# Both layers of a channel MLP by Strassen's seven block products on one Trainium2 core

## The chip, the cores and the metric

The kernel runs on 1 core of one Trainium2 chip. TensorE does the matrix products and the transposes, VectorE (DVE), ScalarE (ACT) and GpSimd (POOL) everything between them; SyncE (SP) issues every DMA. The metric is the device time of one execution in microseconds. Time before: 950.23 us, the median of 3 runs (949.29 to 950.75). What a measurement of this kernel can tell from no change is about 0.2%, some 2 us.

## The reference, cut to what matters

```python
# q, k, v: (4, 12, 448, 64); 4 * 448 = 1792 tokens of 12 * 64 = 768 numbers
x  = attention(rmsnorm(q), rmsnorm(k), v)             # softmax, 48 heads
h  = relu(x @ moe_w_in)                               # 768 -> 1024, split in u, v
x  = (u * (w_spatial @ norm(v) + b)) @ moe_w_out      # 512 -> 768
u  = x + token_mlp(x)                                 # over tokens, 448 -> 256 -> 448
h2 = relu(u @ moe2_w_ch1) @ moe2_w_ch2                # 768 -> 1536 -> 768
return u + h2
```

The weights arrive as 64-bit floats. The last but one line is the channel MLP that is changed.

## The kernel before, in words

Every product of full precision is made from three TensorE passes: each operand is split into a rounded high part and the remainder (`HI`, `LO`), and `PASSES` multiplies high by high, high by low and low by high.

A weight of 64 bits goes through `convert` (line 495 on): ACT takes the absolute value, DVE clamps, shifts and merges the two words in four instructions, ACT makes the high part and POOL subtracts it for the low part. Weights that are wanted more than once are converted early, by `prepare_uo` and `prepare_next`, in pieces of 128x256 beside the attention, and stored in scratch tensors (`wu_d`, `wo_d`, `w1_d`, `w2_d`, and two blocks each of the channel layers, `c1_d`, `c2_d`).

The stages: attention, 24 pairs of heads in slots of eight softmax maxima each (`nm`), with the gated MLP (`moe`) of the first three batches laid between; `moe` of the last batch with the first products over tokens; the token MLP (`Tokens`); and the channel MLP (`channels`). In `channels` the hidden layer is made in six groups of two blocks of 128 features. For each group and each of four token blocks (512, 512, 512, 256) `up` makes two hidden blocks (18 matmuls each, tile `h2ps`, split again by ACT and DVE), and `down` multiplies the previous ones by the second layer and adds them on DVE to sums of all 1792 tokens that stay in SBUF (`acc`, tile `o_ps`). Each group's weights are fetched as 64-bit words and converted in this stage (`word`, `c`).

The order of instructions on each engine is not written by hand. The kernel records operations (`Plan.add`) with an estimated cost (`Plan.estimate`), and `Plan.issue` places them with `Plan.place`: at each step the engine that comes free first takes its most urgent ready operation. Operations of DVE and POOL that need the SBUF port the two share (`op.port`) exclude one another there. `successors` opens new pools in SBUF when all users of the old ones are done (a fence).

Of the kernel before, what the change touches and what calls it, by code (L numbers as in the profile page):

```python
# [149 lines left out]
class Plan:  # L150
# [63 lines left out]
    def estimate(self, engine, fn, out, ins, kwargs):  # L214
# [30 lines left out]
        return max(475, size / 260), 2400 + 1.2e-3 * size  # L245
# [17 lines left out]
    def place(self, before, after, lag, weight, tiles=None):  # L263
# [21 lines left out]
        while placed < len(ops):  # L285
            t, e = min(
                (free_at[e] if waiting[e] else max(free_at[e], due[e][0][0]), e)
                for e in engines if waiting[e] or due[e])
            while due[e] and due[e][0][0] <= t:
                i = heapq.heappop(due[e])[1]  # L290
                heapq.heappush(waiting[e], (weight[i], i))
            i = heapq.heappop(waiting[e])[1]
            if e == "tensor" and ops[i].parts != parts:

                near = [x for x in waiting[e] if ops[x[1]].parts == parts and x[0] <= weight[i] + NEAR]
                if near:
# [4 lines left out]
                    i = x[1]  # L301
            if ops[i].port:
# [110 lines left out]
SWITCH, NEAR = 75, 2500  # L413

# [23 lines left out]
def attention_moe_mixer(  # L438
# [97 lines left out]
    c1_d = [scratch([P, 2, KD, P], F32R, f"c1_d{f}") for f in range(2)]  # L536
    c2_d = [scratch([P, 2, DM], F32R, f"c2_d{f}") for f in range(2)]
# [48 lines left out]
    class Attention:  # L586
# [131 lines left out]
        def divisors(self, i):  # L718
# [5 lines left out]
            wide = p.tile([T, 2 * C, D], F32, tag="wide", bufs=1, name="wide")  # L724
# [191 lines left out]
    def prepare_next(mp):  # L916
# [25 lines left out]
        n = NX // P  # L942
        for f in range(2):
            for j in range(0, KD, n):
                piece(
                    wdram(w_ch1)[j * P:(j + n) * P, f * P * W:(f + 1) * P * W].rearrange(
                        "(j p) f -> p j f", p=P), P, (n, P), c1_d[f][:, :, j:j + n])
                yield
        for f in range(2):
            for t in range(0, DM, NX):  # L950
                piece(wdram(w_ch2)[f * P:(f + 1) * P, t * W:(t + NX) * W], P, (NX,), c2_d[f][:, :, t:t + NX])
                yield
# [95 lines left out]
    class Tokens:  # L1048
# [6 lines left out]
        def prepare(self):  # L1055
            p = self.p
            self.w1 = p.tile([P, 2 * C - 1, DT], F32R, tag="w1", bufs=1, name="w1")
            self.w2 = p.tile([P, 2, KT, S], F32R, tag="w2", bufs=1, name="w2")
            self.w2r = p.tile([P, KT, 2, R], F32R, tag="w2r", bufs=1, name="w2r")
# [9 lines left out]
            fetch(self.w2, w2_d)  # L1069
            for kt in range(KT):  # L1070
                for a in (HI, LO):
                    fetch(self.w2r[:, kt, a], w2_d[:, a, kt, LAST:])
# [32 lines left out]
        def sums(self, b, n):  # L1105
            ns = slice(n * self.N, (n + 1) * self.N)
            for c, (t, m) in enumerate(TOK):
                ps = mm_tile("u_ps")[:, :self.N]
                x = self.x[b, c][:m, ns]
                if m == P:  # L1110
                    yield from run(
                        ps, [(self.w2[:, w, kt, t:t + m], self.h1[b, n, kt][:, a])
                             for kt in range(KT) for a, w in PASSES], 6)
                else:
                    yield from run(
                        ps, [(self.w2r[:, kt].rearrange("p a t -> p (a t)"), self.h1[b, n, kt][:, a])
                             for kt in range(KT) for a in (HI, LO)], 6)
                    two = self.p.tile([R, self.N], F32, tag="two", bufs=1, name="two")
# [5 lines left out]
        def turn(self, b, n, ut):  # L1124
            for j in range(n * KD // 2, (n + 1) * KD // 2):

                tp = psum.tile([P, C * P], "tp", "tp")
                for c, (t, m) in enumerate(TOK):
                    nc.tensor.transpose(tp[:, t:t + P], self.x[b, c][:, j * P:(j + 1) * P], ident)
                tpf = tp[:, :S]  # L1130
                bs = slice(b * S, (b + 1) * S)
# [10 lines left out]
    def channels(wp, cp, ut):  # L1142
        blocks = [(t0, min(512, NTOK - t0)) for t0 in range(0, NTOK, 512)]
        out_f = out.rearrange("b s d -> (b s) d")
        G = 2
        c1, c2 = {}, {}
        N = DM // 2

        def load_up(f):
            t = wp.tile([P, 2, KD, P], F32R, tag="c1", bufs=3, name="c1")  # L1150
            c1[f] = t
            if f < 2:
                nc.sync.dma_start(out=t.bitcast(F32), in_=c1_d[f].bitcast(F32))
                return
            for i in range(2):
                js = slice(i * KD // 2, (i + 1) * KD // 2)
# [147 lines left out]
    for _ in tokens():  # L1304
        pass
# [35 lines left out]
```

## Time and profile before

| | |
|---|---|
| median of 3 runs | 950.23 us (949.29 to 950.75) |
| span of the profiled execution, first to last instruction | 947.7 us, 2.5 us under that median |
| granted TensorE clock, mean | 0.996 |
| PE busy | 915.4 us, 97% of the span |
| DVE / ACT / POOL busy | 568.6 / 454.2 / 340.9 us |
| attention up to its last softmax maximum | 0 to 441.5 us |
| last batch's gated MLP, first token products | to 535.2 us |
| token MLP | to 595.5 us |
| channel MLP | to the end |

The span is that of one execution under the profiler; the profile gives no other time for it. Busy time is counted per engine, so one may be compared with the length of a stretch. A busy PE is not PE at its peak, since the ends of matmuls are modelled: the rate is read from long runs of one matmul in the chain of waits.

### The profile page before, as it was taken

To read this page: it belongs to the slowest core of one execution; us is meant where nothing else is said; L and a number is where in the kernel's file an instruction comes from. 1 tells how busy PE (TensorE), PEld (TensorE's weight loads), DVE (VectorE), ACT (ScalarE), POOL (GpSimd) and SP (SyncE) were. 2 spreads that over 40 slices of the span, in tenths; PEclk is the share of its full clock that TensorE was granted. 3 is DMA by queue.
4 is the path that set the end of the run, shared out by engine and by line. 5 is a ranking of instruction groups with operands and counts; after the bars stand their busy time and mean duration, and the time that the engine had idled before them with its cause. 6 is when DMAs were issued, how large, how long until landed. Compare 5 with 4: busy or idle time off the path is not lost.

```text
span 947.7 us, 15541 instructions
## 1 busy us (share of the span) xinstructions
PE 915.4 (97%) x5368; PEld 741.9 (78%) x5368; DVE 568.6 (60%) x1235; ACT 454.2 (48%) x1145; POOL 340.9 (36%) x501
## 2 busy tenths in 40 slices
PE   4897999999999999999999999999999999999998
PEld 2444467778667786677899999899899999999898
DVE  4888888876776666764151376634655556565434
ACT  5897887777776666675342344301312212122100
POOL 2566445685557654656044123101201102011100
PEclk9999999999999999999999999999999999999999
DMA  6455645557524565233764385721211112111024
GB/s 145 138 146 145 173 134 145 134 173 218 142 63 129 182 202 152 67 107 122 240 205 155 100 275 162 270 90 34 84 51 45 57 34 84 51 51 50 17 89 144
DMA packets 124654, 118.58 MB, mean 125 GB/s; under 512 B 74784, under 2 KB 108128, under 8 KB 123040
## 3 DMA queue, kind: packets, MB, share of 16 engines
q1 hardware_dynamic: 124576, 117.59, 41.2%
q8 instruction: 42, 0.69, 0.3%
q14 instruction: 36, 0.29, 0.1%
HBM read 89.77 MB, written 27.79 MB: 124 GB/s over the span
## 4 chain that ended last, share of the span: by engine, by line
PE 89%; ACT 4%; DMA 2%; DVE 2%; SPq 1%; issue 1%; POOL 0%; ACTq 0%; DVEq 0%; POOLq 0%
PE o_ps L406 19%; PE h2ps L406 18%; PE tp L406 10%; PE av L406 8%; PE sc L406 6%; PE xps L406 6%; PE ups L406 6%; PE vps L406 6%; PE sps L406 4%; PE u_ps L406 3%; PE h1ps L406 3%; ACT e L406 2%; SPq L406 1%; DVE wpart L406 1%; ACT et L406 1%
## 5 line engine op out<-in xcount | busy, mean ns | idle before, releaser
L406 PE MATMUL o_ps<-c,h 128*128 128x384 f32 x1008 | 179.8, 337 | 0.0
L406 PE MATMUL h2ps<-ut,c 128*128 128x512 f32 (+1 forms) x864 | 179.4, 364 | 0.0
L406 PEld LDWEIGHTS o_ps<-c,h 128*128 128x128 f32 x1008 | 175.0, 188 | 2.1 <-DVE acc L406 0.5
L406 PEld LDWEIGHTS h2ps<-ut,c 128*128 128x128 f32 x864 | 148.0, 189 | 24.1
L406 POOL TENSOR_TENSOR c<-word,c 128x384 fp32r<-128x384 f32 x40 | 40.6, 1014 | 271.7 <-ACT c L406 248.2
L406 ACT ACTIVATE e<-sc,nm 112x448 f32<-112x448 f32 x192 | 120.9, 640 | 36.4 <-PE tp L406 19.7
L406 DVE TENSOR_REDUCE nm<-sc 112x1 f32<-112x448 f32 x192 | 110.3, 615 | 41.4 <-PE sc L406 41.2
L406 PE MATMUL tp<-ident,e 112*128 112x112 f32 x672 | 96.2, 265 | 4.9 <-DVE et L406 2.6
L406 PEld LDWEIGHTS tp<-ident,e 112*128 112x128 f32 x672 | 74.1, 142 | 30.9 <-ACT et L406 7.8
L406 DVE TENSOR_TENSOR acc<-o_ps,acc 128x384 f32<-128x384 f32 x140 | 77.3, 555 | 29.5 <-PE o_ps L406 28.8
L406 POOL TENSOR_SCALAR e<-e,sums 112x448 f32<-112x448 f32 x112 | 70.7, 649 | 46.7 <-DVE sums L406 14.5
L406 ACT ACTIVATE c<-word 128x384 fp32r<-128x384 f32 x40 | 21.0, 525 | 128.3 <-DVE word L406 63.6
L406 ACT ACTIVATE h<-h2ps 128x512 fp32r<-128x512 f32 (+1 forms) x48 | 25.9, 539 | 111.6 <-PE h2ps L406 111.2
L406 DVE SCALAR_TENSOR_TENSOR h<-h2ps,h 128x512 fp32r<-128x512 f32 (+1 forms) x48 | 30.0, 625 | 80.6 <-ACT h L406 80.5
L406 ACT ACTIVATE et<-tp 128x448 f32<-128x448 f32 x120 | 65.5, 552 | 18.6 <-PE tp L406 16.8
L406 PE MATMUL ups<-xp,wu 128*128 128x448 f32 x288 | 70.2, 379 | 0.3 <-PE tp L406 0.3
L406 PE MATMUL av<-et,v 128*64 128x448 f32 x288 | 67.3, 564 | 0.2 <-DVE kt L406 0.2
L406 PE MATMUL xps<-wo,g 128*128 128x256 f32 x432 | 62.6, 291 | 0.4 <-ACT xo L406 0.4
L406 PEld LDWEIGHTS xps<-wo,g 128*128 128x128 f32 x432 | 55.0, 190 | 5.3 <-issue 1.3
L406 PEld LDWEIGHTS ups<-xp,wu 128*128 128x128 f32 x288 | 51.6, 188 | 8.3 <-issue 2.1
L406 PE MATMUL vps<-wv,xp 128*128 128x512 f32 x216 | 56.6, 405 | 1.0 <-ACT e L406 1.0
L406 DVE TENSOR_SCALAR word<-word 128x384 f32<-128x384 f32 (+2 forms) x92 | 33.7, 368 | 36.2 <-ACT word L406 34.3
(113 smaller groups left out, 1458.5 us busy)
## 6 DMA issues: line engine op xcount, KB each, us to landing
raw<-in_moe_w_ch_dram SPq DMA_DIRECT2D x40, 384.0 KB, 3.2
wu<-wu_d SPq DMA_DIRECT2D x16, 768.0 KB, 4.6
wo<-wo_d SPq DMA_DIRECT2D x12, 1024.0 KB, 5.1
raw<-in_q_dram SPq DMA_DIRECT2D x48, 112.0 KB, 2.8
acc<-u_d SPq DMA_DIRECT2D x14, 384.0 KB, 7.8
out_dram<-o SPq DMA_DIRECT2D x28, 192.0 KB, 1.9
v<-in_v_dram SPq DMA_DIRECT2D x48, 96.0 KB, 2.7
x_d<-xo SPq DMA_DIRECT2D x36, 128.0 KB, 2.3
```

The costliest lines, as they stand in the source:

```text
L406: getattr(getattr(self.nc, op.engine), fn)(*args, **kwargs)
```

## The change

Three parts.

**Products.** Each layer is taken as 2 by 2 blocks, and the eight block products are replaced by seven (`PRODUCTS`). Tokens split into batches 0, 1 and 2, 3, the inner dimension and the output columns in halves. `up` now makes, for each product and batch of the half, one split operand (`operand`: ACT the high part, DVE the remainder, 128x1344) and six blocks of 9 matmuls over 448 tokens, which DVE adds into four hidden tiles (`c11` to `c22`); ACT applies the ReLU in SBUF. `down` makes per product seven operands of 128x768 and 18 matmuls of 384 columns for each. The sums of activation blocks that products 3 and 4 need are made in place by POOL (`sums`). `fetch` brings a product's weights (2.36 MB) into a ring of two buffers.

**Weights.** Seven sums of weight blocks per layer are made ahead and kept in scratch. `blocks_ch1` does the first layer beside the attention: nine groups, each with four words of 128x256 to convert and seven splits (four with a subtraction on POOL before). `plain_ch2` converts two of the second layer's blocks in 24 pieces of 128x192 beside the last batch's gated MLP, and `mixed_ch2` the other five in six groups of 128x384 beside the token MLP and `up`. The twelve pieces for the channel layers in `prepare_next` go.

**Order.** `Plan.estimate` gives long DMAs a higher rate, and `Plan.place` lets DVE and POOL yield the shared port to the more urgent of the two. `turn` no longer splits `ut`; the tile `two` moves to the pool that opens at the last fence; the token MLP's second weight is one tile.

```diff
-        return max(475, size / 260), 2400 + 1.2e-3 * size
+        return max(475, size / (380 if n >= 512 else 260)), 2400 + 1.2e-3 * size
@@ Plan.place
+            other = SHARED.get(e)
+            if ops[i].port and port <= t and other in due and free_at[other] <= t:
+                ...
+                if waiting[other] and waiting[other][0][0] < weight[i] and ops[waiting[other][0][1]].port:
+                    heapq.heappush(waiting[e], (weight[i], i))
+                    e = other
+                    i = heapq.heappop(waiting[e])[1]
@@ prepare_next
-        for f in range(2):
-            for j in range(0, KD, n):
-                piece(
...
+    def blocks(pool, src, dst, n, i, c, w, tags):
...
+        def split(k, x, y=None, keep=True):
+            t = pool.tile([P, 2, w], F32R, tag=part, bufs=2, name="part")
+            lo = t[:, LO].bitcast(F32)
+            if y is not None:
+                to = x if keep else lo
+                nc.gpsimd.tensor_tensor(to, x, y, op=ALU.subtract)
+                x = to
+            nc.scalar.activation(t[:, HI], x, AF.Copy)
+            nc.vector.tensor_tensor(t[:, LO], x, t[:, HI].bitcast(F32), op=ALU.subtract)
+            at0 = i * cols + c
+            nc.sync.dma_start(out=dst[k][:, :, at0:at0 + w].bitcast(F32), in_=t.bitcast(F32))
...
@@ Tokens.turn
-                nc.scalar.activation(ut[j][:, HI, bs], tpf, AF.Copy)
-                nc.vector.tensor_tensor(
-                    ut[j][:, LO, bs], tpf, ut[j][:, HI, bs].bitcast(F32), op=ALU.subtract)
+                nc.scalar.activation(ut[b * 2 // B, n][:, b % (B // 2), j], tp[:, :S], AF.Copy)
@@ in place of channels
+    def sums(x, s):
+        (x11, x12), (x21, x22) = x
+        def put(to, a, b, op=ALU.subtract):
+            nc.gpsimd.tensor_tensor(s(to), s(a), s(b), op=op)
+        def s2():
+            put(x21, x21, x22, ALU.add)
+            put(x11, x21, x11)
+            return s(x11)
+        def s3():
+            put(x12, x12, x11)
+            put(x11, x22, x11)
+            return s(x11)
...
+    PRODUCTS = (("A11", B11), ("A12", B21), ("S2", T2), ("S3", T3), ("S1", T1), ("S4", B22), ("A22", T4))
...
+    def up(wp, chan, ut):
...
+        for name, k in PRODUCTS:
+            w = chan.pop(k, None) or fetch(wp, c1_d[k])
+            for b in range(B // 2):
+                op = operand(wp, [P, 2, JH, S], "op", 2, first[b][name])
+                for f in range(KH):
+                    ps = psum.tile([P, 512], "sc", "h2ps")[:, :S]
+                    yield from run(
+                        ps, [(w[:, h, j * FH + f * P:j * FH + (f + 1) * P], op[:, a, j])
+                             for j in range(JH) for a, h in PASSES], 100)
...
+    def down(wp, keep):
...
+        for n, (name, k) in enumerate(PRODUCTS):
...
+            w = fetch(wp, c2_d[k])
+            for m in range(M):
+                make = sums(hs[0], lambda x, m=m: x[:, :, m * P:(m + 1) * P])[name]
+                pool, tag, bufs = (wp, "op", 2) if ops % 3 < 2 else (keep, "h", 1)
...
+                op = operand(pool, [P, 2, KH, P], tag, bufs, make)
+                ps = psum.tile([P, 512], "sc", "o_ps")[:, :DH]
+                if name in places:
...
+                    nc.gpsimd.tensor_tensor(u, u, old, op=ALU.add)
+                yield from run(
+                    ps, [(op[:, a, f], w[:, h, f * DH:(f + 1) * DH]) for f in range(KH) for a, h in PASSES], 100)
...
```

Three places in the order, before and after. On PE, the middle of the channel MLP before, where `h2ps` (first layer, from `ut` and weights `c`) and `o_ps` (second layer, from hidden blocks `h`) alternate:

```order
L406 MATMUL h2ps<-ut_7210,c_8090 128x512 x3
L406 MATMUL h2ps<-ut_7231,c_8090 128x512 x3
L406 MATMUL o_ps<-c_7786,h_8218 128x384 x3
L406 MATMUL o_ps<-c_8271,h_8241 128x384 x3
L406 MATMUL o_ps<-c_7786,h_8218 128x384 x3
```

and from the end of the token MLP (transposes `tp`) to the end of the program after it:

```order
L418 MATMUL h2ps<-op,w 128x448 x24
L418 MATMUL tp<-ident,x_8108 128x128
L418 MATMUL h2ps<-op,w 128x448 x2
L418 MATMUL tp<-ident,x_8108 128x128
L418 MATMUL h2ps<-op,w 128x448 x2
L418 MATMUL tp<-ident,x_8065 128x128
L418 MATMUL tp<-ident,x_8082 128x128
L418 MATMUL tp<-ident,x_8094 128x128
L418 MATMUL tp<-ident,x_8108 128x128
L418 MATMUL h2ps<-op,w 128x448 x726
L418 MATMUL o_ps<-w,op 128x384 x882
```

The layers now stand one behind the other: with the two matmuls ahead of these rows there are 756 and 882 of them, in place of 864 and 1008 that alternate.

On DVE, a place in the attention's last third before (`nm` the softmax maxima, `wpart` a weight piece, `lrz`, `lry`, `vr` the norm of the gated MLP, `et`, `kt`, `qt` evictions of transposes):

```order
L406 TENSOR_REDUCE nm<-sc 112x1 x2
L406 TENSOR_TENSOR qt<-tp,qt 128x448
L406 TENSOR_SCALAR lrz<-lrz 128x1
L406 SCALAR_TENSOR_TENSOR wpart<-raw,wpart 128x256
L406 TENSOR_TENSOR lry<-lry,lrz 128x1
L406 TENSOR_SCALAR sums<-sums 112x4
L406 TENSOR_SCALAR vr<-vr,mv,lry 128x512
L406 RECIPROCAL sums<-sums 112x4
L406 COPY et<-tp 128x448
L406 TENSOR_REDUCE nm<-sc 112x1
```

and one in the same third after (`half` a word of `blocks_ch1`, `part` its split):

```order
L418 TENSOR_TENSOR part<-half,part 128x256
L418 TENSOR_SCALAR half<-half 128x256 x4
L418 SCALAR_TENSOR_TENSOR half<-raw,half 128x256 x4
L418 TENSOR_REDUCE nm<-sc 112x1 x2
L418 TENSOR_TENSOR part<-half,part 128x256
L418 TENSOR_SCALAR sums<-sums 112x4
L418 TENSOR_SCALAR vr<-vr,mv,lry 128x512
L418 RECIPROCAL sums<-sums 112x4
L418 TENSOR_REDUCE nm<-sc 112x1
```

One converted piece between two pairs of maxima has become two whole words and two splits, ten instructions ahead of or between them.

On POOL, the last rows before (`c`, low parts of weights of the channel layers):

```order
L406 TENSOR_TENSOR c_9785<-word,c_9785 128x384 x2
L406 TENSOR_TENSOR c_9881<-word,c_9881 128x384 x2
L406 TENSOR_TENSOR c_10026<-word,c_10026 128x384 x2
L406 TENSOR_TENSOR c_10205<-word,c_10205 128x384 x2
L1335 UNCONDITIONAL_BRANCH
```

and those around the start of `down` after (`c_9038`, `c_8642`, `c_9232` the hidden tiles `c21`, `c11`, `c22`; `o_9780` is `o12`):

```order
L418 TENSOR_TENSOR half_9145<-half_9145,h 128x384
L418 TENSOR_TENSOR c_9038<-c_9038,c_9232 128x6x128 x2
L418 TENSOR_TENSOR c_8642<-c_9038,c_8642 128x6x128
L418 TENSOR_TENSOR c_9038<-c_9038,c_9232 128x6x128
L418 TENSOR_TENSOR c_8642<-c_9038,c_8642 128x6x128
L418 TENSOR_TENSOR c_9038<-c_9038,c_9232 128x6x128
L418 TENSOR_TENSOR c_8642<-c_9038,c_8642 128x6x128
L418 TENSOR_TENSOR u<-u,o_9780 128x384 x2
L418 TENSOR_TENSOR c_8642<-c_9038,c_8642 128x6x128
```

POOL's work at the end of the program was splitting weights; it is now the sums of hidden blocks, made ahead of products 3 and 4 and before the additions to `u`.

## Rows read from the trace of the kernel before

**Rows 1.** The page: its span and its first part.
```profile
span 947.7 us, 15541 instructions
PE 915.4 (97%) x5368; PEld 741.9 (78%) x5368; DVE 568.6 (60%) x1235; ACT 454.2 (48%) x1145; POOL 340.9 (36%) x501
```

**Rows 2.** Stretches: engines' busy time and instructions, PEclk, DMA share, GB/s.
```profile
15.80:132.60 116.80, 102.31 (x570) 52.02 (x566) 94.83 (x208) 99.28 (x273) 64.14 (x99) 0.97 0.56 150
230.90:441.50 210.60, 208.61 (x1335) 151.92 (x1335) 139.94 (x344) 146.40 (x401) 123.13 (x205) 1.00 0.46 134
441.50:535.20 93.70, 93.29 (x577) 83.44 (x574) 25.32 (x54) 33.13 (x76) 29.03 (x29) 1.00 0.53 172
535.20:595.50 60.30, 60.30 (x375) 58.92 (x375) 41.99 (x74) 26.57 (x51) 16.48 (x12) 1.00 0.62 208
595.50:947.70 352.20, 348.58 (x1877) 321.77 (x1875) 185.99 (x375) 67.82 (x130) 40.53 (x40) 1.00 0.23 76
144.00:168.00 24.00, 24.00 (x146) 17.48 (x146) 20.39 (x54) 19.38 (x53) 11.22 (x17) 1.00 0.62 167
600.00:624.00 24.00, 24.00 (x121) 21.19 (x120) 13.48 (x26) 5.27 (x11) 2.04 (x2) 1.00 0.78 282
```

**Rows 3.** Chain of waits, 690 to 735 us: start, length, what.
```profile
694.41 4.32 PE h2ps L406 x36
698.73 8.32 PE o_ps L406 x48
707.06 8.20 PE h2ps L406 x36
```

**Rows 4.** Groups by form, channel layers: line, engine, op, tiles, forms, count | busy, mean ns | idle.
```profile
L406 PE MATMUL o_ps<-c,h 128*128 128x384 f32 x1008 | 179.8, 337 | 0.0
L406 PE MATMUL h2ps<-ut,c 128*128 128x512 f32 x648 | 152.2, 391 | 0.0
L406 PE MATMUL h2ps<-ut,c 128*128 128x256 f32 x216 | 27.2, 283 | 0.0
```

**Rows 5.** Groups by form: one weight piece in the attention stage.
```profile
L406 ACT ACTIVATE wpart<-raw 128x256 f32<-128x256 f32 x41 | 18.4, 448 | 3.6 <-DMA c_d<-wpart 2.1 <-DMA wo_d<-wpart 1.4
L406 ACT ACTIVATE wpart<-wpart 128x256 fp32r<-128x256 f32 x41 | 17.4, 433 | 3.5 <-DVE wpart L406 3.2
L406 DVE TENSOR_SCALAR wpart<-wpart 128x256 f32<-128x256 f32 x41 | 16.0, 395 | 3.0 <-ACT wpart L406 3.0
L406 DVE TENSOR_SCALAR wpart<-wpart 128x256 uint32<-128x256 uint32 x41 | 14.0, 346 | 0.4
L406 DVE SCALAR_TENSOR_TENSOR wpart<-raw,wpart 128x256 uint32<-128x256 uint32 x82 | 37.4, 467 | 0.7 <-DVE wpart L406 0.2
L406 POOL TENSOR_TENSOR wpart<-wpart 128x256 fp32r<-128x256 f32 x41 | 31.2, 762 | 46.0 <-ACT wpart L406 46.0
L406 DVE SCALAR_TENSOR_TENSOR wpart<-raw,wpart 128x192 uint32<-128x192 uint32 x4 | 2.1, 524 | 0.0
```

**Rows 6.** Groups by form: evictions and splits after it.
```profile
L406 DVE TENSOR_TENSOR ut<-tp,ut 128x448 fp32r<-128x448 f32 x24 | 14.5, 619 | 2.2 <-ACT ut L406 1.9
L406 DVE TENSOR_TENSOR acc<-o_ps,acc 128x384 f32<-128x384 f32 x140 | 77.3, 555 | 29.5 <-PE o_ps L406 28.8
L406 ACT ACTIVATE xh<-x 128x768 fp32r<-128x768 f32 x16 | 13.1, 841 | 4.5 <-PE h1ps L406 3.8 <-DMA x<-x_d 0.5
L406 POOL TENSOR_TENSOR c<-word,c 128x384 fp32r<-128x384 f32 x40 | 40.6, 1014 | 271.7 <-ACT c L406 248.2 <-issue 11.8 <-PE o_ps L406 11.6
```

**Rows 7.** Order of time, 575.5 to 580 us, DVE and POOL: start, length, what.
```profile
574.06 1.86 POOL L406 TENSOR_TENSOR xh<-x,xh 128x768 fp32r<-128x768 f32 x1 [2.84 <-ACT xh L406]
576.13 0.95 DVE L406 TENSOR_TENSOR xh<-x,xh 128x768 fp32r<-128x768 f32 x1
576.52 2.25 POOL L406 TENSOR_TENSOR xh<-x,xh 128x768 fp32r<-128x768 f32 x1 [0.60 <-ACT xh L406]
577.73 1.87 DVE L406 TENSOR_TENSOR xh<-x,xh 128x768 fp32r<-128x768 f32 x1 [0.65 <-ACT xh L406]
```

More of the change, by code (lines that the diff above doesn't have):

```diff
@@ L941, in prepare_next @@
                 yield
[L942 to L952 removed]
+    B11, B21, T2, T3, T1, B22, T4 = range(7)
@@ new lines, in blocks, with word, split @@
+    def blocks(pool, src, dst, n, i, c, w, tags):
+        cols = src.shape[1] // (2 * W)
+        raw, half, part = tags
+        pair = pool.tile([P, 2, w], F32, tag=f"{half}0", bufs=1, name="half")
+        third = pool.tile([P, w], F32, tag=f"{half}1", bufs=1, name="half")
+        def word(r, q, t):
+            at0 = (q * cols + c) * W
+            rows = (r * n + i) * P
+            x = weights(pool, raw, 2, src[rows:rows + P, at0:at0 + w * W], P, (w,))
+            convert(pool, None, 0, x, P, w, None, None, at=t.bitcast(U32))
+            return t
+        def split(k, x, y=None, keep=True):
+            t = pool.tile([P, 2, w], F32R, tag=part, bufs=2, name="part")
+            lo = t[:, LO].bitcast(F32)
+            if y is not None:
+                to = x if keep else lo
+                nc.gpsimd.tensor_tensor(to, x, y, op=ALU.subtract)
+                x = to
+            nc.scalar.activation(t[:, HI], x, AF.Copy)
+            nc.vector.tensor_tensor(t[:, LO], x, t[:, HI].bitcast(F32), op=ALU.subtract)
+            at0 = i * cols + c
+            nc.sync.dma_start(out=dst[k][:, :, at0:at0 + w].bitcast(F32), in_=t.bitcast(F32))
+        b11 = word(0, 0, pair[:, 0])
+        split(B11, b11)
+        yield
+        b12 = word(0, 1, pair[:, 1])
+        yield
+        b22 = word(1, 1, third)
+        split(B22, b22)
+        yield
+        split(T3, b22, b12, keep=False)
+        split(T1, b12, b11)
+        yield
+        split(T2, b22, b12)
+        yield
+        b21 = word(1, 0, pair[:, 0])
+        split(B21, b21)
+        yield
+        split(T4, b22, b21)
+        yield
@@ new lines, in blocks_ch1, with plain_ch2, mixed_ch2, get @@
+    def blocks_ch1(mp):
+        for i in range(JH):
+            for c in range(0, FH, NX):
+                yield from blocks(mp, wdram(w_ch1), c1_d, JH, i, c, NX, ("wraw", "half", "wpart"))
+    def plain_ch2(mp):
+        for i in range(KH):
+            for c in range(0, DH, NX // 2 * 3 // 2):
+                yield from plain(mp, wdram(w_ch2), c2_d, KH, i, c, NX // 2 * 3 // 2, ("wraw", "wpart"))
+    def mixed_ch2(wp, keep):
+        def get(tag, n, bufs):
+            return (keep if tag == "h" else wp).tile([P, n], F32, tag=tag, bufs=bufs, name=tag)
+        for i in range(KH):
+            yield from mixed(get, wdram(w_ch2), c2_d, KH, i, DH)
@@ L1302, in tokens, with before_up @@
             yield from tok.turn(b, 1, ut)
-    for _ in tokens():
-        pass
-    cp, = successors([tok.p], late, (ctx, "chan", "right"))
-    channels(wp, cp, ut)
+    chan = {}
+    def before_up():
+        for k in (B11, B21):
+            chan[k] = fetch(wp, c1_d[k])
+        yield from tokens()
+        chan["pool"], = successors([tok.p], late, (ctx, "chan", "right"))
+    merge(
+        (chain(before_up(), up(wp, chan, ut)), 8 * B * 9 + 14 * KH, 0, 1),
+        (mixed_ch2(wp, keep), 6 * KH, 0.1, 0.9))
+    for _ in down(wp, keep):
+        pass
     nc.issue(psum)
```

261 lines of the change are left out of this document (153 added, 108 removed).

## The prediction

> **What bounds the kernel now.** I read the page's first part, then the stretches between the stages, then the chain of waits in the channel MLP. The page has PE busy for 915.4 of 947.7 us, the next engine (DVE) for 568.6 [rows 1]. The stretches say where that holds [rows 2]. From 595.5 us on, the channel MLP, PE works 348.58 us with DVE busy 53% and POOL 12% of the time; in the token MLP PE is busy 60.30 of 60.30 us; in the attention's last half (230.9 to 441.5) 208.61 of 210.6, and there DVE (139.94), ACT (146.40) and POOL (123.13) are all loaded. Only the attention's start, where nothing can be laid between the softmax steps, leaves PE idle, 14.5 of 116.8 us. In the channel MLP the chain is PE alone, one run of matmuls behind the other [rows 3]: whatever takes matmuls away there shortens the end, as long as the new work of the other engines keeps up, and as long as what is moved forward, into the attention, finds room there.
>
> **Products: what goes.** From the chain [rows 3], 36 matmuls of 512 columns take 8.20 us, 0.228 each; 36 of 256 columns 4.32, 0.120; 48 of 384 columns 8.32, 0.1733. The counts are those of the groups [rows 4]: 648 x 0.228 + 216 x 0.120 + 1008 x 0.1733 = 147.7 + 25.9 + 174.7 = 348.3 us, which is the 348.58 us of the stretch [rows 2]. After, the order has 756 matmuls of 448 columns and 882 of 384. 448 columns lie on the line between 256 and 512: 0.120 + 192 x 0.108 / 256 = 0.201 us. 756 x 0.201 + 882 x 0.1733 = 152.0 + 152.9 = 304.9 us. That is **-43.5 us**, all on the path, and the surest term; the loads of weights into the array keep their form and number per matmul.
>
> **First layer's weights, beside the attention.** One word of 128x256 costs ACT 0.448, DVE 0.395 + 0.346 + 2 x 0.467 = 1.675 us [rows 5]; a split costs ACT 0.433 and, with a subtraction, POOL 0.762. A 256-column subtraction from SBUF on DVE has no row; 768 columns took 0.95 [rows 7], a third is 0.32, the two-input form of a word 0.467; I take 0.42. Nine groups are 36 words and 63 splits: DVE 60.3 + 26.5, ACT 16.1 + 27.3, POOL 36 x 0.762 = 27.4 us. The 12 pieces that go gave back 20.1, 10.6 and 9.1. So DVE +66.7, ACT +32.8, POOL +18.3 us. By the order all but two words and six splits (some 6 us) stand ahead of the last softmax maximum, so DVE comes to about 139.9 + 61 = 201 of the 210.6 us, 95%; by the shortest prices (0.32 a split, fewer waits in a word) some 90%. DVE's queue is in order: behind each word wait the maxima, for which ACT's exponentials and then PE's transposes wait. What covers it is PE's other work between, the gated MLP. The trace has DVE at 85% with PE busy 24.00 of 24.00 us (144 to 168 us), and nothing denser at full PE [rows 2]. The upper bound is the attention's start, where DVE at 81% and ACT at 85% leave PE 87.6% busy: 208.61 / 0.876 = 238.1, +27.5 us. The lower is a gain, since the rules of order could shorten the 14.5 idle us: -4. I take **+9**: nearer the row at 85%, with about half of what lies above it (201 - 179 = 22 us) lost.
>
> **Two blocks of the second layer, beside the last batch.** 24 pieces of 192 columns: DVE under 24 x 1.675 = 40 us on top of 25.32 of 93.7, POOL 24 x 0.762 = 18 at most on 29.03 [rows 2, 5]: covered. DMA gets 24 x 2 x 0.197 MB = 9.4 MB more, 100 GB/s on 172; at 282 GB/s PE was busy throughout [rows 2]. What may be late is a load of the gated MLP's weights that stands on SP behind a store of a piece: 0 to 6, taken **+2**, since those loads are issued two blocks ahead.
>
> **Token MLP.** 24 DVE subtractions of 0.619 [rows 6] go; they were covered, so nothing is gained. The tile `two` now waits for the fence, on which `ut` waited already. Loads of two weight blocks (4.7 MB) and the first groups of `mixed_ch2` share the queue. -1 to 4, taken **+1**.
>
> **Up.** One operand feeds 54 matmuls, 10.9 us. It asks, by width from 768 columns [rows 6, 7], 0.841 x 1.75 = 1.5 us of ACT and 0.95 x 1.75 = 1.7 of DVE; two buffers give a whole operand's time for it. A bank's 9 matmuls last 1.81 us; DVE adds it in 0.62 (twice in product 5). `mixed_ch2` has 30 conversions and splits in place of 40 splits before. A product's weights are 2.36 MB in 21.8 us: 8.4 us at 282 GB/s, 17.6 at the attention's 134 [rows 2]. All under cover: 0 to 5, taken **+1**.
>
> **Down.** Per operand PE has 18 x 0.1733 = 3.12 us; ACT needs 0.841, DVE 0.95 and one addition of 0.555 [rows 6, 7]. For products 1 to 4 (28 operands, 87.4 us) POOL makes 28 sums of 768 columns and 7 additions of 384. Here the shared port decides. In order of time [rows 7] a POOL subtraction that began while DVE's was running ended 1.69 us after DVE (576.13 + 0.95 to 576.52 + 2.25), and the next of DVE ended 0.83 us after POOL (578.77 to 579.60): they took turns. Taking turns, 28 x (1.69 + 0.83) + 7 x 0.86 (half of 1.69) = 76.6 of 87.4 us. That fits, at 88%, with three sums ahead of `down` by the order, and three operand buffers; if each has its full length (1.86 alone, 0.95), 28 x (1.86 + 0.95) + 7 x 1.014 = 85.8 us, still under. 0 to 10, taken **+2**. Products 5 to 7 have no sums and are free of it. The last addition and store are as before.
>
> The Trainium skill (SBUF — State Buffer, Who interferes with whom) speaks against putting this work on these two engines: the port pair that DVE and GpSimd share is an exclusive lock, and the loser blocks entirely for an instruction that takes two SBUF inputs. The rows just read agree, 0.95 us alone and 1.87 beside POOL. By that rule alone the sum for `down` would be the 76.6 to 85.8 us above, no more than PE's, so it moves nothing there; in the attention it is the mechanism of rival (1).
>
> **Sum.** 947.7 - 43.5 + 9 + 2 + 1 + 1 + 2 = 919.2 us of span; the median of the runs stands 2.5 us over the span of the profiled execution, so **922 us**. With the attention's loss anywhere between 0 and 18 us this case spans 910 to 932.
>
> **The rivals.** (1) *The attention becomes bound by DVE and the port.* POOL has 123.1 + 18.3 = 141 us in the stretch, and DVE's words and splits stand 80 us on the same port: 221 of 210.6 us if each holds it for its whole record. For it: [rows 7]. Against: records are longer than the hold (0.95 against 0.83), and the planner knows the port. It gives the bound of 27.5 in place of 9: 941. (2) *Slower than before: the conversions stand in the softmax chain.* If each DVE instruction of a word delays the maxima behind it and the gated MLP runs out as filler, the added DVE time is paid in full, 66.7 in place of 9: 980. It decides from 37 us of the 66.7 on, where the saving is spent. Against: in the order 60 matmuls of the gated MLP (`xps`) still stand together behind the attention's last one, as before, so the filler lasts. (3) *Weights come late.* If `mixed_ch2`'s stores hold SP and a product's 2.36 MB needs 23.5 us in place of 21.8, each of 14 products waits 1.7 us: +24, 946. Against: 282 GB/s [rows 2]. (4) *The rules of order help.* If half of the start's 14.5 us comes back and the denser part costs nothing: 922 - 9 - 7 = 906.
>
> **How the numbers follow.** Forecast 60%, (1) 20, (2) 6, (3) 4, (4) 10. Predicted 922. The range 905 to 942 holds the forecast, most of (4) and two thirds of (1), 8 in 10. A measurement of this kernel can tell about 0.2% (2 us) from no change. Faster by more: the forecast, (4), and nearly all of (1) and (3), 0.92. Slower: (2) and a piece of (1), 0.06. Same 0.02.
>
> **What would show it.** `h2ps` at 0.201 and `o_ps` at 0.173 us in unbroken runs prove the first term, and a layer takes 152 to 155 us. PE's idle in the stretch up to the last maximum shows the second: under 5 us if (4), about 10, or near 30 with DVE over 95% busy if (1). In `down`, PE waiting for DVE's `op` in products 3 and 4 means that the port term was too small; waiting for a DMA of `w` means (3). I am wrong if the layers' PE time is not near 305 us, or if the attention ends more than 30 us later.

## The result and the profile after

The changed kernel took **962.97 us** (median of 4 runs, 958.78 to 965.78) beside 950.31 for the kernel before on the same chip: ratio 1.0142, 95% interval 1.0110 to 1.0174. It is 1.4% slower; 922 us was forecast, in a range of 905 to 942. The profiled execution of after, the shortest of the four, took 958.78 us with a span of 957.0, 9.3 us over the span of before.

The page's span and first part, to be held against [rows 1], and the row of the granted clock (40 slices, tenths of full speed):

```profile
span 957.0 us, 16041 instructions
...
PE 888.3 (93%) x5134; PEld 722.5 (76%) x5134; DVE 694.3 (73%) x1364; ACT 542.8 (57%) x1312; POOL 507.9 (53%) x609
...
PEclk9998999999999999998989999998999999999999
```

PE's work fell by 27.1 us (915.4 to 888.3), not by 43.5, and its idle time (span less busy) rose from 32.3 to 68.7 us, by 36.4: together the 9.3. The mean granted clock fell from 0.996 to 0.980. That is at most 15.3 us of a span (0.016 of 957, if PE was bound all through), beside the 16.4 us that are missing of the 43.5. The stretches, to be held against [rows 2] (from 230.9 us to the last softmax maximum, to the last `xps`, to the last `u_ps`, to the end of `up`, to the end); the last two rows come back below:

```profile
230.90:461.20 230.30, 212.97 (x1313) 152.10 (x1312) 195.81 (x464) 162.06 (x451) 144.71 (x213) 0.99 0.63 190
461.20:572.00 110.80, 104.32 (x622) 93.05 (x621) 62.80 (x159) 52.33 (x134) 49.72 (x62) 0.95 0.73 236
572.00:637.60 65.60, 59.70 (x350) 55.37 (x349) 42.61 (x75) 33.77 (x64) 26.30 (x21) 0.97 0.84 282
637.60:800.40 162.80, 158.16 (x769) 144.78 (x768) 113.14 (x159) 68.24 (x110) 66.51 (x43) 0.98 0.61 211
800.40:957.00 156.60, 153.17 (x884) 152.83 (x882) 93.32 (x97) 42.97 (x55) 83.97 (x52) 1.00 0.42 144
484.00:490.50 6.50, 4.00 (x34) 3.80 (x32) 2.63 (x6) 3.12 (x7) 3.40 (x4) 1.00 0.74 237
490.50:497.30 6.80, 5.32 (x19) 4.74 (x20) 1.85 (x7) 1.89 (x6) 1.18 (x2) 0.50 0.90 296
```

The attention's end is 19.7 us later (230.3 for 210.6), the last batch's stretch 17.1 longer (110.8 for 93.7). From there to the end it took 385.0 us, where 412.5 stood before: 27.5 gained. 19.7 + 17.1 - 27.5 = 9.3. The gain sits where it was looked for; the attention and the stretch behind it, ahead of any product, gave it all back and more. How the loss of 36.8 us divides between the two depends on the order (fourth group).

The products themselves are what they were said to be. From the chain of waits, one piece in `up` and one in `down` at full clock (start, length, what), and both groups of the page, for [rows 3, 4]:

```profile
654.85 55.95 PE h2ps L418 x276
...
819.92 30.16 PE o_ps L418 x174
```
```profile
L418 PE MATMUL h2ps<-op,w 128*128 128x448 f32 x756 | 157.7, 370 | 4.6 <-DVE x L418 3.3
...
L418 PE MATMUL o_ps<-w,op 128*128 128x384 f32 x882 | 153.1, 334 | 0.0
```

55.95 / 276 = 0.203 us and 30.16 / 174 = 0.1733 (forecast: 0.201 and 0.1733). In `down` PE never waits.

**Where PE stops.** Before, all of PE's stops from 441 us to the end came to some 0.4 us. Now there are stops of 2 to 4 us there and ahead of it. Three are shown. First, the last batch, from the chain of waits (start, length, what):

```profile
484.89 0.41 POOL xr L418
...
486.02 0.61 POOL part L418
...
486.65 4.45 DMA c_d<-part
...
491.20 0.30 ACT part L418
...
491.54 0.39 ACT xo L418
...
491.98 2.93 PE xps L418 x12
```

and ACT in order of time at this stop and at one of 2.04 us that ended at 564.4 (start, length, engine, instruction, [idle before]):

```profile
488.49 0.84 ACT L418 ACTIVATE xh<-x 128x768 fp32r<-128x768 f32 x1 [1.54 <-DMA x<-x_d]
...
491.20 0.37 ACT L418 ACTIVATE part<-raw 128x192 f32<-128x192 f32 x1 [1.60 <-DMA c_d<-part]
...
561.94 0.37 ACT L418 ACTIVATE part<-raw 128x192 f32<-128x192 f32 x1 [3.95 <-DMA c_d<-part]
```

A piece of `plain_ch2` starts with ACT writing into the tile `part`. The ring has two, so this instruction waits until the store of the piece two before has landed. The store took 4.45 us from its issue, and ACT stood idle for the last 1.60 of them (3.95 at the second stop). ACT takes its instructions in order; behind it stands the eviction `xo`, and for that waits the next `xps`: PE stood still for 3.98 us ahead of 491.98. The ring is not all of that stop: just before, ACT had waited 1.54 us for a load of `x`, with the same eviction behind it.

Second, `up`'s start, DVE and then POOL in order of time (start, length, engine, instruction, [idle before]):

```profile
636.90 1.55 DVE L418 TENSOR_TENSOR op<-ut,op 128x1344 fp32r<-128x1344 f32 x1
638.36 6.31 DVE L418 SCALAR_TENSOR_TENSOR half<-s,half 128x384 uint32<-128x384 uint32 x1
644.60 0.54 DVE L418 TENSOR_TENSOR x<-u_ps,x 64x384 f32<-64x384 f32 x1
```
```profile
638.24 1.07 POOL L418 TENSOR_TENSOR x<-two,x 64x384 f32<-64x384 f32 x1 [1.84 <-ACT two L418]
639.27 3.08 POOL L418 TENSOR_TENSOR ut<-ut 128x1344 f32<-128x1344 f32 x1
642.32 1.93 POOL L418 TENSOR_TENSOR h<-h 128x384 f32<-128x384 f32 x2
```

The instruction of DVE that took 6.31 us takes 0.55 when POOL is quiet. POOL's run of four began just ahead of it and ended at 644.25, and DVE's ended at 644.67: by these records it waited out the run. Behind it stood the eviction of the last `u_ps`, and for that PE waited 3.25 us. Third, the same in the attention:

```profile
306.59 3.17 DVE L418 TENSOR_SCALAR half<-half 128x256 f32<-128x256 f32 x1
309.69 0.61 DVE L418 COPY et<-tp 128x448 f32<-128x448 f32 x1
```
```profile
306.63 0.64 POOL L418 TENSOR_SCALAR e<-e,sums 112x448 f32<-112x448 f32 x1
307.23 1.02 POOL L418 TENSOR_TENSOR g<-tg,g 128x384 fp32r<-128x384 f32 x1
308.20 0.33 POOL L418 TENSOR_TENSOR rest<-tg,rest 128x64 fp32r<-128x64 f32 x1
308.48 1.13 POOL L418 TENSOR_TENSOR tg<-tg,tv 128x448 f32<-128x448 f32 x1
```

3.17 us for 0.28; the copy `et` behind it is late, and PE stops for 2.19 us. Taken over all of DVE's instructions from 240 us to the last maximum, the time above the shortest record of the same tiles and form was 13.7 us before and 37.1 after.

Not every run of POOL holds DVE up for its whole length. In `down` POOL makes five sums without a gap, 827.78 to 839.78 us, and a split on DVE with two operands in SBUF (0.95 us when POOL is quiet) begins and ends in their midst:

```profile
827.78 12.00 POOL L418 TENSOR_TENSOR c<-c,c 128x768 f32<-128x768 f32 x5
```
```profile
835.92 2.16 DVE L418 TENSOR_TENSOR op<-c,op 128x768 fp32r<-128x768 f32 x1 [0.26 <-ACT op L418]
```

What decides between the two cases no run shows.

**The clock.** The last two rows of the stretches show what a stop costs besides: in the 6.5 us in which the 3.98 us stop lies the clock is granted in full, in the next 6.8 us half (1.2 of 2.4 GHz). After the stops of 3.15 (at 427 us), 2.04 and 3.25 us it fell in the same way, and after six stops of 0.4 to 0.8 us within 13 us (573 to 585); after the one of 2.19 us in the attention it did not. That is 27 us at half clock behind 240 us; before had none there. The Trainium skill (TensorE: Matmul & The Clock Gate, What's actually happening) says that the clock is granted by how busy PE has been; the trace agrees, and the prediction had no term for it.

### The profile page after: what moved, and what is told of

Its sections match the earlier page's. It is cut to its first block, busy times and chain, and to the rows that moved or that the text cites. A ratio compares the mean times of both kernels' runs of the same rounds, so it can differ in the third digit from the quotient of the medians.

```text
span 957.0 us, 16041 instructions
## 1 busy us (share of the span) xinstructions
PE 888.3 (93%) x5134; PEld 722.5 (76%) x5134; DVE 694.3 (73%) x1364; ACT 542.8 (57%) x1312; POOL 507.9 (53%) x609
## 4 chain that ended last, share of the span: by engine, by line
PE 44%; DVE 7%; DMA 6%; ACT 3%; issue 3%; POOL 1%; SPq 0%; ACTq 0%; POOLq 0%; DVEq 0%
PE o_ps L418 16%; PE h2ps L418 14%; DMA c_d<-part 4%; PE xps L418 2%; PE u_ps L418 2%; PE tp L418 2%; PE ups L418 2%; PE vps L418 2%; DVE part L418 1%; DVE half L418 1%; PE av L418 1%; PE h1ps L418 1%; PE sps L418 1%; DMA x_d<-xo 1%; DMA x<-x_d 1%
## 5 line engine op out<-in xcount | busy, mean ns | idle before, releaser
L418 PE MATMUL h2ps<-op,w 128*128 128x448 f32 x756 | 157.7, 370 | 4.6 <-DVE x L418 3.3
L418 PEld LDWEIGHTS h2ps<-op,w 128*128 128x128 f32 x756 | 142.9, 190 | 17.7 <-DVE x L418 3.6
L418 PE MATMUL o_ps<-w,op 128*128 128x384 f32 x882 | 153.1, 334 | 0.0
L418 PEld LDWEIGHTS o_ps<-w,op 128*128 128x128 f32 x882 | 152.9, 188 | 0.0
L418 ACT ACTIVATE op<-c 128x768 fp32r<-128x768 f32 x49 | 41.6, 848 | 102.7 <-PE o_ps L418 101.4
L418 DVE TENSOR_TENSOR op<-c,op 128x768 fp32r<-128x768 f32 x49 | 68.8, 1405 | 22.7 <-ACT op L418 22.7
L418 DVE TENSOR_TENSOR c<-c,h2ps 128x448 f32<-128x448 f32 x84 | 50.6, 617 | 32.9 <-PE h2ps L418 32.8
L418 ACT ACTIVATE et<-tp 128x448 f32<-128x448 f32 x120 | 64.8, 548 | 16.4 <-PE tp L418 14.6
L418 POOL TENSOR_TENSOR c<-c,c 128x768 f32<-128x768 f32 x28 | 58.7, 2119 | 26.1 <-ACT c L418 23.1
L418 DVE TENSOR_TENSOR part<-half,part 128x256 fp32r<-128x256 f32 (+1 forms) x78 | 45.2, 582 | 18.1 <-ACT part L418 17.9
L418 POOL TENSOR_TENSOR u<-u,o 128x384 f32<-128x384 f32 x28 | 34.7, 1249 | 43.6 <-DVE o L418 30.4
```

Of the source, the lines that this page charges most:

```text
L418: getattr(getattr(self.nc, op.engine), fn)(*args, **kwargs)
```

## The experiments

Ratios are to the kernel before, run on the same chip in turn. Most edits make the planner write another order, so that was an experiment too (the fourth group). PE's idle time is a page's span less its busy time.

**First group: the preparation of the weight blocks left out.** The loads, conversions, sums and splits go; the stores stay, from one constant tile. Of `no_ch1` (the two others alike, `no_weights` has all three):

```diff
 def blocks_ch1(mp):
+    t = mp.tile([P, 2, NX], F32R, tag="wpart", bufs=2, name="part")   # filled from ident
     for i in range(JH):
         for c in range(0, FH, NX):
-            yield from blocks(mp, wdram(w_ch1), c1_d, JH, i, c, NX, ("wraw", "half", "wpart"))
+            for k in range(7):
+                nc.sync.dma_start(out=c1_d[k][:, :, i * FH + c:i * FH + c + NX].bitcast(F32), in_=t.bitcast(F32))
```

> The changed kernel, with the preparation of both layers' weight blocks left out (no loads of the weights, no conversions, no sums, no splits; the stores into scratch stay, from one constant tile, so the result is not the reference's). Theory A: the products save 43.5 us as forecast, and all that was lost (about 56 us against 963) is the preparation's work on DVE, POOL, ACT and their queues: the time falls to 907 (903 to 912), with the last softmax maximum back at 439 to 443 us, the last xps at about 535, and up at 152 to 155 us. Rival B: the mended rules of order, not the work, cost the time: over 940. Rival C: what stands around the seven products themselves (sums and splits of the operands on the shared port in up, a lower granted clock) costs some of it: 912 to 925, with up still above 158 us.

> Only the first layer's weight blocks beside the attention are left out (their stores stay, from a constant tile; result not the reference's). Theory A: it gives back the 19.6 us by which the last softmax maximum was late, and nothing behind it changes: 941 to 945. If the attention is late for another reason (rules of order, Rival B): 955 or more, the last maximum still past 453 us. If the part of the loss is only that above the forecast's 9 us: about 953.

> Only the two plain blocks of the second layer beside the last batch's gated MLP are left out (their stores stay, from a constant tile; result not the reference's). Theory A: the stretch from the last maximum to the last xps goes from 111 to about 95 us, and the total to 944 to 950. If that stretch is late because the attention leaves it fewer matmuls ready and not because of the 24 pieces, the total stays above 955.

> Only the other five blocks of the second layer beside the token MLP and up are left out (their stores stay, from a constant tile; result not the reference's). Theory A: the token MLP's stretch goes from 65.6 to about 62 us and up from 162.8 to 153 to 155, so the total to 948 to 953. Rival C, that up loses its 10.8 us to its own sums and splits on the port that DVE and POOL share: up stays at 158 or more, the total at 957 to 961.

| kernel | us | ratio (95%) | PE idle | clock | last maximum |
|---|---|---|---|---|---|
| changed kernel | 962.97 | 1.0142 (1.0110 to 1.0174) | 68.7 | 0.980 | 461.2 |
| no_weights | 909.80 | 0.9602 (0.9581 to 0.9623) | 40.0 | 0.996 | 443.8 |
| no_ch1 | 925.14 | 0.9766 (0.9721 to 0.9811) | 49.3 | 0.991 | 449.0 |
| no_plain | 937.75 | 0.9896 (0.9867 to 0.9925) | 50.9 | 0.991 | 445.5 |
| no_mixed | 956.05 | 1.0096 (1.0064 to 1.0127) | 69.4 | 0.979 | 472.2 |

The page and the stretches of `no_weights` (the attention from 230.9 us, the last batch, the token MLP, `up`):

```profile
span 909.0 us, 14878 instructions
...
PE 869.0 (96%) x5134; PEld 713.4 (78%) x5134; DVE 518.9 (57%) x983; ACT 480.3 (53%) x1139; POOL 411.0 (45%) x513
```
```profile
230.90:443.80 212.90, 210.01 (x1334) 152.00 (x1334) 124.14 (x294) 140.40 (x384) 116.38 (x193) 1.00 0.66 202
443.80:532.00 88.20, 87.03 (x545) 79.22 (x542) 19.99 (x52) 32.66 (x74) 26.58 (x28) 1.00 0.53 169
532.00:596.80 64.80, 62.08 (x377) 60.26 (x376) 29.52 (x48) 28.91 (x57) 18.45 (x13) 0.97 0.94 322
596.80:752.60 155.80, 154.88 (x770) 143.09 (x769) 71.90 (x100) 53.35 (x78) 31.68 (x13) 1.00 0.39 139
```

Theory A holds in the main: with the products alone, and the new rules of order, the kernel is 4.0% faster, 38 us of the 43.5. The preparation costs 5.4% (1.0142 - 0.9602), some 51 us. `up` takes 155.8 us without it and 162.8 with it, so Rival C is out. `no_mixed` says the same: its `up` takes 154.6. But the parts don't add as Theory A had it: `no_ch1` came 16 us under its range, `no_plain` 6 under, `no_mixed` 3 over. 3.8% + 2.5% + 0.5% is more than 5.4%, and two runs that change nothing ahead of the last maximum moved it, `no_plain` 15.7 us forward and `no_mixed` 11.0 back. In `no_plain` the order fills the room: with the plain pieces gone, part of the first layer's blocks moves behind the maximum (DVE's time on `half` ahead of it from 240 us on falls from 79.3 to 62.4 us). The two jobs compete for the same stretch, 230.9 to 572 us. At its end, the last `xps`, they nearly add: 535.2 us before, 572.0 in the changed kernel, 548.8 in `no_ch1`, 551.7 in `no_plain`, 532.0 in `no_weights`. Up to there the first layer's preparation costs 23 us, the two plain blocks 20, and the two together 40.

**Second group: DVE's load, or the port.** `no_sub` leaves out POOL's subtractions between blocks, `no_clamp` DVE's first instruction of each word; `dve_sub` and `pool_clamp` move the one and the other to the other engine.

```diff
-                nc.gpsimd.tensor_tensor(to, x, y, op=ALU.subtract)      # no_sub: gone
+                nc.vector.tensor_tensor(to, x, y, op=ALU.subtract)      # dve_sub
...
-            nc.vector.tensor_scalar(a.bitcast(F32), a.bitcast(F32), least, most, ALU.max, ALU.min)   # no_clamp: gone
+            nc.gpsimd.tensor_scalar(a.bitcast(F32), a.bitcast(F32), least, most, ALU.max, ALU.min)   # pool_clamp
```

> In the changed kernel the 60 subtractions that POOL makes between weight blocks (36 of 256 columns beside the attention, 24 of 384 beside the token MLP and up; about 50 us of POOL) are left out, and DVE's and ACT's work stays as it is (the blocks stored are then the wrong ones). Theory P, POOL's runs of work on the port shared with DVE hold up DVE's instructions, with the softmax maxima and copies behind them: 940 to 948; DVE's time above the shortest record of each kind (29.8 us from 240 us to the last maximum, 17.8 in up) falls below 18 and below 9. Theory L, DVE simply has more work than fits, whoever shares its port: 955 to 962.

> The opposite: DVE's first instruction of each word of the two layers' weights (the limits put on the number, 72 instructions, about 34 us of DVE) is left out; POOL's subtractions stay. The numbers here lie inside the limits, so nothing else changes. Theory L: 935 to 945, the more so as the attention's DVE falls from 86% to 80%. Theory P: the collisions stay, 948 to 956.

> All of the work is done, but the 60 subtractions between weight blocks run on DVE (0.41 us for 256 columns) in place of POOL (0.76). Theory P: fewer collisions outweigh 15 + 13 us more of DVE: 945 to 957. Theory L: DVE has even more to do: 968 to 985.

> All of the work is done, but the limits on the words of the two layers' weights are set by POOL in place of DVE. Theory L: 940 to 952. Theory P: POOL's runs get longer and what DVE gains it loses waiting: 958 to 975.

`no_sub` 953.36 us, 1.0053 (1.0025 to 1.0081); `no_clamp` 963.42, 1.0182 (1.0136 to 1.0228); `dve_sub` 957.53, 1.0109 (1.0074 to 1.0145); `pool_clamp` 975.92, 1.0302 (1.0272 to 1.0331). Theory L's 935 to 945 for `no_clamp` is missed by 18 us and more: 72 instructions of DVE went, and nothing was won. `no_sub` and `dve_sub` lie between the two theories' ranges. In `no_sub` DVE's time above the shortest record fell by 11.0 us in the attention (37.1 to 26.1) and by 6.2 in `up` (18.5 to 12.3), a little less than Theory P had asked, and the time by much less. Groups of the attention's `half` on DVE (count, shortest/median/longest ns), of the changed kernel and then of `no_clamp`:

```profile
L418 DVE TENSOR_SCALAR half<-half x67: 258/289/3170, 241.2 to 461.1; 128x256 f32<-128x256 f32 x34, 128x256 uint32<-128x256 uint32 x33
L418 DVE SCALAR_TENSOR_TENSOR half<-raw,half x66: 409/420/1261, 242.4 to 458.1; 128x256 uint32<-128x256 uint32 x66
```
```profile
L418 DVE SCALAR_TENSOR_TENSOR half<-raw,half x72: 407/420/2220, 249.1 to 475.6; 128x256 uint32<-128x256 uint32 x72
L418 DVE TENSOR_SCALAR half<-half x36: 261/288/1989, 248.3 to 473.2; 128x256 uint32<-128x256 uint32 x36
```

The medians lie close to the shortest, the longest are many times that. In `no_clamp` the last maximum came at 480.5 us, 19.3 later than in the changed kernel, with all 72 instructions ahead of it; `after_near` below puts it at 480.6 with nothing left out, so the order can have eaten the gain. Theory P isn't shown either: `no_clamp` missed its 948 to 956 too, and `pool_clamp` is confounded, since the limits cost POOL 1.06 us a word where DVE needs 0.29:

```profile
L418 POOL TENSOR_SCALAR half<-half x34: 1060/1062/1146, 246.1 to 472.7; 128x256 f32<-128x256 f32 x34
```

What was measured: 86 us more on POOL went with 15 us more in all, 72 instructions less on DVE with no gain. `no_sub`'s 8.5 us and `dve_sub`'s 3 are no larger than what another order does (below).

**Third group: the ring of two, and the rules of order.** `plain3` gives the pieces of `plain_ch2` a third buffer, the tile `half0`, idle there:

```diff
-            t = pool.tile([P, 2, w], F32R, tag=part, bufs=2, name="part")
+            tag, bufs = (("wpart", 2), ("wpart", 2), ("half0", 1))[turn[0] % 3]
+            turn[0] += 1
+            t = pool.tile([P, 2, w], F32R, tag=tag, bufs=bufs, name="part")
```

`plain3_dve` adds `dve_sub`. `before_rules` is the kernel before with the four edits of the rules; `after_norules` and `plain3_norules` are without them.

> The changed kernel with three buffers instead of two for the pieces of the second layer beside the last batch (the third is a tile that lies idle there). All of the work is done. Theory M: PE's stops of 3.98 and 2.04 us there come from pieces that wait for the store of the one two before, in ACT's queue ahead of the evictions of the gated MLP; with a third buffer the stretch from the last maximum to the last xps falls from 111 to 98 to 102 us and the total to 950 to 955. If the shared port alone makes the loss: 960 to 965, the stretch above 108.

> Three buffers and the 60 subtractions between weight blocks on DVE in place of POOL. If the two causes are separate and add up: 942 to 949. If they are the same loss seen twice: 953 to 958.

> The kernel before with the mended rules of order alone (the transfer's price by width, the engine's clock moved on before it chooses, the port offered to the other engine). Theory Q, the rules alone are worth little: within 5 us of before, 943 to 951. If they explain part of the loss: above 953. If, as the prediction's rival (4) has it, they win back half of the attention's idle start: 935 to 942.

> The changed kernel with the old rules of order. If the mended rules are what makes the added work fit at all: 975 to 1000. If they harm: below 955. If they are worth little here too: 958 to 968.

`plain3` took 944.73 us, 0.9973 (0.9949 to 0.9996), 1.7% under the changed kernel, by its own interval just faster than before. That is a larger gain than Theory M's 950 to 955, while the stretch in which the buffer was to work, 103.5 us, missed its 98 to 102. `plain3_dve` 950.88, 1.0038 (1.0020 to 1.0056): the subtractions on DVE now cost 6 us instead of saving 3; both lie within what another order does. The page of `plain3`, its row of the granted clock, and its first three stretches:

```profile
span 939.1 us, 16046 instructions
...
PE 881.7 (94%) x5134; PEld 715.3 (76%) x5134; DVE 687.8 (73%) x1364; ACT 543.6 (58%) x1312; POOL 510.2 (54%) x609
...
PEclk9899999999999999999999999999999999999999
```
```profile
230.90:458.10 227.20, 213.42 (x1328) 153.12 (x1327) 195.37 (x468) 164.41 (x452) 148.65 (x219) 1.00 0.63 190
458.10:561.60 103.50, 98.44 (x596) 86.34 (x594) 62.24 (x159) 51.22 (x133) 46.51 (x58) 1.00 0.80 256
561.60:622.60 61.00, 57.18 (x346) 54.00 (x347) 37.42 (x71) 31.98 (x61) 24.61 (x19) 1.00 0.81 284
```

DVE does the same work (195.4 us for 195.8 in the attention), but no stop of PE behind 240 us is longer than 1.87 us, and there is no stretch of half clock behind 240 us at all in this execution (940.87 us; in the nine others the mean clock was 0.989 to 0.994). Of the 17.9 us between the two spans, 11.3 are idle time (68.7 to 57.4) and 6.6 PE's busy time (888.3 to 881.7), which half clock lengthens (the mean was 0.980, and 0.995 here). By stages the spans differ by 3.1 us up to the last maximum, 7.3 beside the last batch, 4.6 in the token MLP and 2.9 behind it.

`before_rules` took 954.26, 1.0077 (1.0056 to 1.0097): on the old work the order that the rules make costs 7 us. `after_norules` took 958.56, 1.0127 (1.0111 to 1.0143), no worse than with them. With all of the work done its token MLP takes 59.5 us and its `up` 154.5, where the changed kernel has 65.6 and 162.8; `before_rules`, with the old work, has 64.6 in the token MLP, and `no_weights`, with no preparation, 64.8. So these two stages lose by the order too, not by the work beside them alone.

**Fourth group: another order of the same work.** `after_near` and `before_near` change one constant of the planner and nothing else; `plain3_near` and `plain3_near4` do it with the third buffer. `plain3_s8` moves one of nine groups of `blocks_ch1` behind the attention.

```diff
-SWITCH, NEAR = 75, 2500
+SWITCH, NEAR = 75, 2000        # plain3_near4: 4000
```

> The changed kernel with one constant of the planner, NEAR, at 2000 in place of 2500 ns: the same instructions in a slightly other order. If the order's accidents are small: 960 to 966. If they are as large as the planner's own figures for the two orders (it puts this one 4 us later): 955 to 972, and then no difference of under about 8 us between two orders proves a cause.

> The kernel before with the same constant at 2000. Small accidents: within 2 us of before. If the kernel before stands on a lucky order: 950 to 956, as slow as with the mended rules alone, and then those rules are no cause.

> Three buffers for the pieces beside the last batch, and the old rules of order. If the rules cost 4 to 7 us, as the two comparisons so far have it: 937 to 941. If that was an accident of the order: 943 to 952.

> Three buffers, and the ninth group of the first layer's blocks (about 10 us of DVE, 3 of POOL, 4 of ACT) made beside the last batch in place of the attention. If the attention loses in proportion to what it holds above some 70 us of DVE for weights: the last maximum comes 5 to 8 us sooner and the total falls to 937 to 942. If the order pulls that group forward anyway, or the last batch loses what the attention gains: 943 to 949.

> Three buffers for the pieces, and NEAR at 2000 ns, the pair of after_near (968.5). If the third buffer is worth some 15 us whatever the order: 948 to 956. If 944.7 was an accident of one order: 957 to 966.

> Three buffers and NEAR at 4000 ns, a third order of the same work; the planner's own figure for it lies 3 us above that of plain3 and 4 below that of plain3_near. Buffer worth 15 us: 944 to 952. Accident: anywhere from 950 to 966. A stretch of half clock is to be seen behind each stop of PE of over 2 us, and none in an order whose stops stay under that.

| work | ratios of its orders (95%) |
|---|---|
| before | 1, 0.9989 (0.9968 to 1.0009) |
| changed kernel | 1.0142 (1.0110 to 1.0174), 1.0203 (1.0166 to 1.0240) |
| with the third buffer | 0.9973 (0.9949 to 0.9996), 1.0025 (1.0007 to 1.0042), 1.0076 (1.0048 to 1.0103) |
| third buffer, old rules | 1.0082 (1.0050 to 1.0114) |
| third buffer, one group moved | 1.0102 (1.0073 to 1.0131) |

The constant alone moves the changed kernel by 6 us and its three-buffer form by 10 from best to worst, the kernel before by 1; but `before_rules`, also the old work in another order, moved that by 7. With and without the third buffer four orders can be compared: 16 us (NEAR 2500), 17 (2000), 7 (`plain3_dve` against `dve_sub`) and 4 (old rules, where the intervals overlap). All four have one sign, so the buffer is very likely a cause; its size hangs on the order, and 944.73 is the luckiest of them. Nor does it end the waits. In `plain3_near4` PE stopped for 4.09 us because ACT stood at the next piece's load, with `xo` behind it:

```profile
564.29 0.37 ACT L418 ACTIVATE part<-raw 128x192 f32<-128x192 f32 x1 [3.83 <-DMA raw<-in_moe_w_ch_dram]
```

The order also sets where the last maximum falls. The stretches of `after_near` up to it and from there to the last `xps`:

```profile
230.90:480.60 249.70, 229.52 (x1356) 158.37 (x1356) 204.60 (x478) 168.13 (x463) 150.05 (x224) 0.97 0.60 181
480.60:579.50 98.90, 95.00 (x573) 84.79 (x570) 55.97 (x141) 47.16 (x122) 44.89 (x52) 0.98 0.78 246
```

The same work, two buffers, and the attention is 39.1 us late and the last batch 5.2, where the changed kernel had 19.7 and 17.1. Only the sum of the two says what was lost up to there.

Moving a group out of the attention lost 12 us against `plain3`: the last maximum came 4.3 us later (462.4 for 458.1), not sooner. The old rules are no better with the third buffer than the slowest order under the new: the 7 us of `before_rules` can't be carried over to the changed kernel.

The clock's half held: `plain3_near4` fell to half clock after its stops of 4.09 and 2.38 us, not after the one of 2.02; `plain3_near` fell after one of 1.88, where `plain3` did not after 1.87. One stop of 2.19 us in the changed kernel was not followed by it either. The length of a stop alone doesn't decide.

## Why the prediction was wrong

- **Products, -43.5: right.** 0.203 and 0.1733 us a matmul. `no_weights`, the same matmuls at the mean clock of before, has PE busy 46.4 us less (869.0) and gains 38.
- **First layer's weights, +9: mis-sized.** The attention ended 19.7 us late, inside the stated bound of 27.5, but in `after_near` it was 39.1; the fairer measure is `no_ch1`, 23 us up to the last `xps` and 3.8% of the whole. The prices were not too low: DVE's time in the stretch rose by 55.9 us (139.9 to 195.8), where some 61 were forecast. The step that failed is the choice between the bounds by the share of DVE's time: DVE stood at 85% (195.8 of 230.3), the very share of the row on which full cover was argued [rows 2], and PE was idle for 17.3 us, where about 10 was the forecast's own sign. The stops that were followed up point at how long one instruction was held and what stood behind it in the queue.
- **Two blocks beside the last batch, +2: the step that failed most.** 17.1 by the stretch, 20 by `no_plain`. "Covered" was read from sums of DVE and POOL; the hold-up was sought on SP, behind a store. At PE's two longest stops there it stood in ACT's queue, behind a two-buffer ring that waits for a store to land (ACT idle for 1.60 and 3.95 us). A third buffer was worth 4 to 17 us of the whole, by the order.
- **Token MLP +1 and `up` +1: too small.** Token MLP 65.6 us for 60.3, `up` 162.8 for 153; in `up` one stop of 3.25 us from a held-up DVE, the half clock behind it, and 1.24 elsewhere. Neither was sure to be lost: under the old rules the same work takes 59.5 and 154.5. Without `mixed_ch2` the total falls by 0.5%, within an order's accident.
- **`down`, +2: none was lost.** The port's own term was the one place where it cost nothing; that the ring of three for `op` is the reason is likely, but no run changed it. "They took turns" [rows 7] was read from two instructions with gaps between POOL's. It held in `down`, where POOL's sums stand back to back, and not at the stops shown above (6.31 us, 3.17).
- **The clock: no term at all.** At most 15.3 us, as large a bound as the error of any other term. How much of it was paid is not shown: `plain3`, at 0.995, has PE busy only 6.6 us less than after.
- **Rivals.** (1) came nearest: the attention lost 19.7 of its 27.5 us, but DVE was 85% busy there, not over 95% (one stretch of 24 us had 96%). (2)'s price, all of the added DVE time on the path, was not paid. (3) is out: PE waited for no load of weight blocks. (4) is out: in the first 134 us PE's idle time did not shrink (26.3 us before, 29.7 after).
- **Its own marks.** Neither "layers not near 305 us" (157.7 + 153.1 = 310.8, half clock included) nor "attention more than 30 us later" came true. They watched two terms of six; the error lay in others, and in small stops everywhere.

Left open: how much of the attention's loss is the port and how much is plain queueing on three loaded engines (DVE 85%, ACT 70%, POOL 63%). The two runs that were to tell it don't: `no_sub` moved the time by no more than another order does, and `no_clamp` came in an order with the last maximum 19.3 us later.

## What to carry to other kernels

An engine's idle share doesn't show that work is "covered". Look at each added instruction for what it waits for (a ring of two whose release is a store's landing, a load) and for what waits behind it in its engine's queue. Where PE leaves little idle time, add to the sum what its stops may cost at half clock afterwards, and measure a second order of the same work before an effect of 1 or 2% is given to a cause. Before moving 50 us of preparation to win 43, cheapen the preparation.

## What the runs showed of the hardware

- Two instructions of DVE whose operands come from SBUF waited out a whole run of POOL's instructions (6.31 us for 0.55, 3.17 for 0.28, each ending just after the run did). The Trainium skill (SBUF — State Buffer, Who interferes with whom) has the port taken for one whole instruction; at these two it stayed with POOL from one to the next, in `down` DVE got in between (2.16 us for 0.95).
- Four stops of PE of 2.04 to 3.98 us were each followed by 3.4 to 6.8 us at half clock, one of 2.19 us was not. Where PE is bound behind it, such a stop costs about twice its length (an estimate: half of 3.4 or 6.8 us on top of the stop).
- One `tensor_scalar` of 128x256 with two limits took 1.06 us on POOL and 0.29 on DVE.
